# Order of the weight halves for the first batch, and q, k requested ahead of V, in a fused attention and maxout kernel

## Chip, cores and metric

The kernel runs on one core of a Trainium2 chip. The metric is the device time of one execution in microseconds (us), less is better. Profiles are of single executions; their span (first to last instruction) is some 1.8 us shorter than the device time of the same execution.

## The reference, cut to what matters

```python
# q, k, v: [8, 8, 576, 64]
mask = block_i >= block_j                    # blocks of 64 positions
attn = softmax(where(mask, q @ k.T / 8, -1e9))
x = (attn @ v).transpose(0, 2, 1, 3).reshape(4608, 512)
g = maximum(x @ w1, x @ w2)                  # w1, w2: [512, 1024]
out = g @ w_out                              # w_out: [1024, 512]
```

## The kernel before

Attention is worked pair of heads by pair (a "group" g is two pairs; a batch has two groups), in bf16. The second stage (maxout and output projection) has no phase of its own: it is cut into units, and `fill(n)` puts steps of the next unit between the pieces of attention, so that TensorE (PE) has work while DVE, ACT and POOL prepare the next piece. The units form one fixed list. A unit may start when the tokens of its span have been transposed; when the unit at the head of the list may not start, `fill` does nothing. The text calls unit f of span i h(i,f). In the profile's names, ps_o is an attention output before its division, rec and xp the reciprocal and the result of the division, ps_xe and ps_xo the transposes of xp, xT their copy, ps_h a product with w1 or w2, ps_y a row block of the output.

```python
spans = [(0, 256), (256, 320)]               # the two spans of batch 0
spans += [(t0, ...512...) for t0 in range(576, NTOK, 512)]

def h_unit(i, f):                            # 128 of 1024 columns f, span i
    for w_sb in (w1_sb, w2_sb):
        pt = ps_m.tile(...)                  # one of four PSUM banks
        for c in range(4):
            nc.tensor.matmul(pt[:, :w], w_sb[:, c, f*128:(f+1)*128], xT[:, c, t0:t0+w], ...)
        ...                                  # w1: DVE copies to h1;  w2: DVE max(h1, pt) -> g

for i in range(NSPAN):                       # the list
    for f in range(8):
        h(i, f)
        ...
    if i == 1:                               # then ps_y of both spans
        ...

def fill(n):
    while n > 0 and at[0] < len(steps) and steps[at[0]][1] <= done_tokens[0]:
        u, _, cost = steps[at[0]]            # cost 0.5 for 256 columns, 0.625 for 320
        next(u); n -= cost; at[0] += 1
```

The prologue, cut. Every `load_w`, `load_wo`, `load_v` is a transfer issued by POOL that casts to bf16; `load_qk` is issued by SP, released by a small POOL memset ("gated"):

```python
    load_w(256, 256)                         # columns 256..511 of w1 and w2
    ...
    load_w(512, 512)                         # second half of w1 and w2
    ...
    masks_q(1)
    for c in range(3): load_v(1, c)          # V of batch 1
    fill(2)
    load_qk(3, (SP, SP), gated=True)         # q, k of group 3
    burst_q1(2); transposes("q", 2, ...)(); fill(3)
    burst_q2(2); av(0, [2, 3, 4]); fill(1)   # av: attention output, ps_o
    ...
    fill(2); x_out(0, 2, NCH)                # transposes x of group 0 into xT
    ...
    cast("q", 3, pool); cast("k", 3, pool)
    load_qk(4, ...); load_wo(0, 4); load_wo(4, 4)
    fill(3)
    # first turn of the main loop, g == 2
    region(tile_0(a), tile_1(a))
    av(3, [2, 3, 4])                         # last attention output of batch 0
    fill(5)
    x_out(1, 2, NCH)                         # only now span 1 (tokens to 576) may start
    fill(...)
```

The softmax here doesn't subtract the row's maximum and nothing guards it: scores larger than these inputs give would overflow.

## Time and profile before

| | before |
|---|---|
| device time, median of 3 | 282.14 us (282.08 to 282.30) |
| span of the profile | 280.4 us |
| busy: PE, DVE, ACT, POOL | 269.3, 185.7, 139.6, 107.7 us |
| granted PE clock | full |

PE is the engine to watch, and from 18 to 48 us it is fed almost without a break (29.77 of 30.00 us, in the prediction). One more line is needed later, the first matmul of the output projection; columns are start, us from first start to last end, engine, line, operation, operands:

```profile
47.92 0.38 PE L215 MATMUL ps_y<-wo_sb,g 128*128 128x512 bf16 x1
```

I call the time from the first matmul behind the last attention output of batch 0 (28.35 us, the row with x10 in the prediction) to this one **the stretch**: 47.92 - 28.35 = 19.57 us. It is the only part of PE's program that the change permutes.

### The profile page before, as it was taken

The page shows a single profiled execution, that of the slowest core. Times are in us where ns is not written, and L with a number is a line of the kernel's source. Part 1 is how long each engine was busy: PE and PEld are TensorE (multiplying, and loading weights), DVE is VectorE, ACT ScalarE, POOL GpSimd, SP SyncE. Part 2 cuts the span into 40 slices and gives each one's busy share as a digit, 9 for nine tenths or more (in the row PEclk, how much of TensorE's full clock was granted, in tenths as well). Part 3 has the DMA queues.
Part 4 walks back from the last instruction along what each step waited for, and adds up shares of the span by engine and source line. Part 5 has one row for each costly group of instructions (what it writes and reads, how often), then busy time and mean ns, then how long its engine had stood idle before and what let it go on. Part 6 is the DMA issues. An engine that isn't in the chain of part 4 may idle for free.

```text
span 280.4 us, 7767 instructions
## 1 busy us (share of the span) xinstructions
PE 269.3 (96%) x3208; PEld 151.5 (54%) x3253; DVE 185.7 (66%) x386; ACT 139.6 (50%) x194; POOL 107.7 (38%) x271
## 2 busy tenths in 40 slices
PE   7699999999999999999999999999999999999995
PEld 2356766655556455555555554646455644444543
DVE  5967879668887676767667576757655766365430
ACT  3786577667664664655647374664653000100112
POOL 2996446764654625164344625371120000000000
PEclk9999999999999999999999999999999999999999
DMA  7999999979934994479266866175301111111114
GB/s 261 263 219 220 187 244 273 250 148 189 210 42 153 154 156 78 178 82 239 49 208 77 219 75 196 52 81 50 67 5 49 49 54 40 39 75 40 73 41 150
DMA packets 55940, 36.68 MB, mean 131 GB/s; under 512 B 38752, under 2 KB 43232, under 8 KB 55904
## 3 DMA queue, kind: packets, MB, share of 16 engines
q0 software_dynamic: 41728, 7.87, 35.0%
q1 hardware_dynamic: 13760, 27.66, 28.8%
q10 hardware_dynamic: 416, 0.66, 0.7%
q8 instruction: 25, 0.41, 0.6%
q14 instruction: 11, 0.09, 0.1%
HBM read 34.60 MB, written 9.44 MB: 157 GB/s over the span
## 4 chain that ended last, share of the span: by engine, by line
PE 91%; DMA 4%; issue 2%; ACT 1%; DVE 1%; POOL 0%; ACTq 0%
PE ps_h L197 43%; PE ps_y L215 22%; PE ps_o L429 11%; PE ps_s L321 8%; DMA vv<-in_v_dram 2%; PE ps_xe L451 2%; PE ps_qT L303 2%; DMA qraw<-in_q_dram 2%; PE ps_kT L303 2%; ACT aT L345 1%; PE ps_s L339 1%; PE ps_y L231 1%; PE ps_w L292 1%; DVE g L206 0%; POOL vv L133 0%
## 5 line engine op out<-in xcount | busy, mean ns | idle before, releaser
L197 PE MATMUL ps_h<-xT,w_sb 128*128 128x512 bf16 (+3 forms) x605 | 136.2, 357 | 1.7 <-issue 0.3
L345 ACT ACTIVATE aT<-ps_s 128x1024 bf16<-128x1024 f32 (+2 forms) x100 | 96.2, 996 | 17.2 <-PE ps_s L321 16.2
L197 PEld LDWEIGHTS <-w_sb 128*128 128x128 bf16 x640 | 57.8, 98 | 57.4 <-issue 8.1
L204 DVE CAST h<-ps_h 128x512 bf16<-128x512 f32 (+3 forms) x80 | 50.9, 637 | 28.9 <-PE ps_h L197 26.7
L215 PE MATMUL ps_y<-wo_sb,g 128*128 128x512 bf16 x273 | 65.5, 379 | 2.1 <-PE ps_s L321 1.3
L206 DVE TENSOR_TENSOR g<-h,ps_h 128x512 bf16<-128x512 bf16 (+3 forms) x80 | 50.6, 632 | 12.0 <-PE ps_h L197 10.5
L350 POOL MEMSET aT<- 64x128 bf16 x124 | 22.3, 199 | 92.7 <-ACT aT L345 91.3
L221 ACT COPY y<-ps_y 128x512 f32<-128x512 f32 x31 | 18.1, 584 | 70.3 <-PE ps_y L215 56.5
L429 PEld LDWEIGHTS <-aT 128*128 128x128 bf16 x960 | 37.3, 98 | 14.1 <-issue 1.3
L215 PEld LDWEIGHTS <-g 128*128 128x128 bf16 x280 | 26.8, 98 | 30.4 <-issue 1.1
L429 PE MATMUL ps_o<-vv,aT 128*128 128x65 bf16 x960 | 39.9, 194 | 0.3 <-DMA vv<-in_v_dram 0.3
L133 POOL DMA_DIRECT2D vv<-in_v_dram x40 | 33.7, 847 | 0.5
L436 DVE TENSOR_TENSOR xp<-ps_o,rec 128x256 bf16<-128x256 f32 (+1 forms) x64 | 31.4, 491 | 2.2
L321 PE MATMUL ps_s<-qT,kT 64*128 64x64 bf16 (+6 forms) x344 | 31.6, 279 | 1.1 <-ACT kT L310 0.7
L435 DVE RECIPROCAL rec<-ps_o 128x4 f32<-128x4 f32 (+1 forms) x64 | 12.0, 188 | 20.6 <-PE ps_o L429 18.9
L310 ACT COPY qT<-ps_qT 128x576 bf16<-128x576 bf16 x15 | 9.6, 638 | 29.4 <-PE ps_qT L303 29.4
L187 POOL COPY g<-g 128x512 bf16<-128x512 bf16 x8 | 4.9, 611 | 38.3 <-DVE g L206 38.2
L129 POOL CAST kn<-kraw 128x1152 bf16<-128x1152 f32 x15 | 17.3, 1151 | 5.2 <-DMA kraw<-in_k_dram 5.1
L129 POOL CAST qn<-qraw 128x1152 bf16<-128x1152 f32 (+1 forms) x15 | 16.5, 1099 | 7.0 <-DMA qraw<-in_q_dram 6.9
L456 DVE COPY xT<-ps_xe 128x640 bf16<-128x640 bf16 (+2 forms) x18 | 8.2, 453 | 15.7 <-PE ps_xe L451 14.9
L310 ACT COPY kT<-ps_kT 128x576 bf16<-128x576 bf16 x15 | 9.6, 638 | 15.0 <-PE ps_kT L303 15.0
L321 PEld LDWEIGHTS <-kT 64*128 64x128 bf16 x344 | 13.2, 95 | 6.6 <-issue 2.8
(44 smaller groups left out, 144.5 us busy)
## 6 DMA issues: line engine op xcount, KB each, us to landing
qraw<-in_q_dram SPq DMA_DIRECT2D x16, 576.0 KB, 4.1
out_dram<-y SPq DMA_DIRECT2D x35, 256.0 KB, 2.1
kraw<-in_k_dram SPq DMA_DIRECT2D x15, 576.0 KB, 5.4
vv<-in_v_dram POOLq DMA_DIRECT2D x32, 128.0 KB, 5.3
w_sb<-in_moe_w_dram POOLq DMA_DIRECT2D x4, 256.0 KB, 6.6
w_sb<-in_moe_w_dram POOLq DMA_DIRECT2D x2, 512.0 KB, 10.7
wo_sb<-in_moe_w_out_dram POOLq DMA_DIRECT2D x2, 512.0 KB, 11.8
kraw<-in_k_dram ACTq DMA_DIRECT2D x1, 576.0 KB, 5.4
```

The source lines that it names most:

```text
L129: copy(out=n[:, j0:j1], in_=t[:, j0:j1])
L133: nc.gpsimd.dma_start(out=vv_r[b % NV][P - rows:, c, :, :D], in_=v[b, :, c * P:c * P + rows, :].rearrange("h p d -> p h d"),)
L197: nc.tensor.matmul(pt[:, :w], w_sb[:, c, f * P:(f + 1) * P], xT[:, c, t0:t0 + w], start=(c == 0), stop=(c == NDM - 1),)
L204: nc.vector.tensor_copy(out=h1[:, :w], in_=pt[:, :w])
L206: nc.vector.tensor_max(g[:, f, m:m + w], h1[:, :w], pt[:, :w])
L215: nc.tensor.matmul(py[:], g[:, f, s * P:(s + 1) * P], wo_sb[:, f, :], start=(f == 0), stop=(f == NFF - 1),)
L310: copies[i](out=t[:, :S].rearrange("q (p j) -> q p j", j=RPP), in_=pts[i].rearrange("q j p -> q p j"),)
L321: nc.tensor.matmul(ps[:, hh, col:col + w], kT[r, k0:k0 + P], qT[r, q0:q0 + w], start=True, stop=True,)
L345: nc.scalar.activation(out=aT_r[p % NA][:, :, a0:a0 + w], in_=ps[:, :, :w], func=AF.Exp, scale=scale,)
L350: (eng or nc.gpsimd).memset(aT_r[p % NA][BLK:, :, a0:a0 + BLK], 0.0)
L429: nc.tensor.matmul(po[:, gi, hh, :], a[:, hh, a0:a0 + P], vv[:, c, h0 + 2 * hh, :], start=(mm == 0), stop=(mm == n_mm - 1),)
L436: nc.vector.tensor_mul(xp[:, ts[0]:ts[0] + n, :, p % 2], po[:, :, :, :D], rec[:, :n].to_broadcast([P, n, 2, D]),)
```

## The change

Intent: for batch 0, use the first half of the columns of w1 and w2 for both spans before the second half of either, so the second half of the weights may land later; and use that freedom to ask for q and k of group 3 earlier, ahead of V of batch 1.

```diff
-        for i in range(NSPAN):
-            for f in range(NFF):
+        for f0 in (0, NFF // 2):
+            for i in range(2):
+                for f in range(f0, f0 + NFF // 2):
+                    h(i, f)
+        for i in range(1, NSPAN):
+            for f in range(NFF if i > 1 else 0):
                 h(i, f)
...
     masks_q(1)
+    load_qk(3, (SP, SP), gated=True)
     for c in range(3):
         load_v(1, c)
     fill(2)
-    load_qk(3, (SP, SP), gated=True)
```

Below, "part 1" is the order of halves, "part 2" the place of the request. After the change all lines behind 253 are numbered five higher.

## The prediction

> **What bounds the kernel now.** I began with the page of the profile. TensorE (PE) is busy 269.3 of 280.4 us and the granted clock is full in every slice, so it is the suspect, but busy is not the same as fed. The table by stage says where it has room (columns: length, then busy us and instruction count of PE, weight loads, DVE, ACT, POOL, then clock, DMA share, GB/s):
>
> ```profile
> 0.00:18.00 18.00, 13.91 (x178) 6.62 (x181) 13.24 (x41) 10.46 (x14) 12.43 (x25) 1.00 1.26 259
> 18.00:48.00 30.00, 29.77 (x495) 21.28 (x493) 23.66 (x57) 21.45 (x29) 18.46 (x47) 1.00 1.35 228
> 48.00:260.00 212.00, 208.32 (x2441) 114.47 (x2480) 142.41 (x278) 104.01 (x146) 76.81 (x200) 1.00 0.54 110
> ```
>
> The change sits in 18 to 48 us, where PE is busy 29.77 of 30.00. DVE has 6.3 us to spare, ACT 8.5, POOL 11.5. The waits of PE from 18 to 275 us, all of them:
>
> ```profile
> PE ps_y L215 <- PE ps_s L321: 1.3, 8, 0.2
> PE ps_y L215 <- issue: 0.6, 4, 0.2
> PE ps_h L197 <- issue: 0.3, 2, 0.2
> PE ps_xo L453 <- DVE kT L310: 0.2, 1, 0.2
> ```
>
> None is for a weight, for q, k or for V. The first three rows repeat in steps of 0.16 to 0.2 us in places where I count a matmul record missing, so even they are mostly not waits. The change, however, is about when w1, w2, q and k are needed and arrive. Is there a wait hidden inside a matmul? I took the spacing of matmuls instead of their busy time:
>
> ```profile
> 28.35 1.25 PE L197 MATMUL ps_h<-xT,w_sb 128*128 128x256 bf16 x10
> 29.54 0.20 PE L451 MATMUL ps_xe<-ident,xp 64*128 64x64 bf16 x1
> ...
> 35.81 2.35 PE L197 MATMUL ps_h<-xT,w_sb 128*128 128x320 bf16 x16
> ```
>
> Ten of 256 columns: (1.25 - 0.27 of the last) / 9 = 0.109 us apart. Sixteen of 320: (2.35 - 0.30) / 15 = 0.137 us. That is the streaming rate of these shapes; nothing hides in them. I shall use 0.109 and 0.137 below. The first row is also where the second half of w1 and w2 is first used (two matmuls finish f=3, eight are f=4), and it streams.
>
> **What the Trainium skill says.** "Perfetto Trace Analysis", section "Identifying the Most-Contended Engine", warns that busy time of matmuls is no measure of how full PE is; hence the spacing. "TensorE: Matmul & The Clock Gate", section "Back-to-back issue gap", gives an isolated gap of N/2.4 + 2.5 ns: 109 ns at 256 and 136 ns at 320, which this trace meets (109, 137). It also gives about 131 ns for a sustained stream at N=512; this trace does not show that (eleven of them in 2.54 us, (2.54 - 0.38)/10 = 216 ns), and the measurement decides. "DMA: Bandwidth & Descriptors", section "Queues, rings and completion order": each DMA engine serves its queues in turn, a packet at a time. So q, k on SP's queue, requested earlier, take their share from the weights waiting on POOL's queue. In the trace before, the second half of w2 took 11.9 us from issue to landing, the first half 6.1 us; that fits sharing but does not prove it.
>
> **The change, part by part.** No instruction is added or removed: PE has 6508 rows in both programs, DVE 386, POOL 184. I compared the PE order. It is the same up to the last attention output (ps_o) of batch 0, which ends near 28.52 us in the trace before, and the same again from the first output-projection matmul (ps_y) at 47.92 us. Only what lies between is permuted, so the change can only win or lose waits in some 20 us, and shift all that follows by that amount.
>
> *Part 1, order of halves.* Work on batch 0's second span needs the transposed x of its tokens, which the transposes x_out(1) make. Before these, the filler may use the first span only. Formerly that was 64 matmuls; now only the 32 of the first half of w come ahead of the second span. The prologue's fills take 30. The fill of 5 behind the last attention output (5 units at cost 0.5: ten matmuls) now finds two. What happens behind that output on DVE, before:
>
> ```profile
> 28.55 0.20 DVE L435 RECIPROCAL rec<-ps_o 128x6 f32<-128x6 f32 x1 [1.18 <-PE ps_o L429]
> 28.79 0.56 DVE L436 TENSOR_TENSOR xp<-ps_o,rec 128x384 bf16<-128x384 f32 x1
> 29.26 0.41 DVE L206 TENSOR_TENSOR g<-h,ps_h 128x256 bf16<-128x256 bf16 x1
> ...
> 30.45 0.35 DVE L456 COPY xT<-ps_xe 128x384 bf16<-128x384 bf16 x1
> 30.71 0.28 DVE L457 COPY xT<-ps_xo 128x256 bf16<-128x256 bf16 x1
> ```
>
> The ten matmuls covered exactly the reciprocal and multiply (xp done at 28.79 + 0.56 = 29.35). Their removal makes two new waits:
> - PE is done with two matmuls at 28.52 + 0.22 = 28.74 and then needs xp. From DVE's end to a PE start I allow 0.06 us (the copy of kT that PE waited for ended at 24.27, PE began at 24.33). x_out starts at 29.41: about 0.67 us empty.
> - x_out is ten short transposes, issued in about 0.2 us, results by 29.8. DVE then copies at 29.85: 0.35, and the second copy, overlapping by 0.08, ends at about 30.40. The next PE work is now h(1,0), which reads those copies: its first two matmuls (the head pairs of x_out(0)) may go at 29.85, the third waits until 30.45. They occupy 2 x 0.137 = 0.27, so about 0.35 us is empty. Before, h(0,5) stood here and needed nothing new; the copies even queued behind other DVE work till 30.45.
>
> Against this: the kernel before loses a little here too. Around x_out its trace has an xo that starts 0.18 us after the first xe, and about 0.2 us between the last transpose and the next h (0.1 of which is the usual changeover). So follow both to the scores of pair 5 behind the k transposes, which begin at 35.45 in the trace before:
> - Before, from 28.52 to 35.45 PE did 34 matmuls of 256 and 7 of 320: 34 x 0.109 + 7 x 0.137 = 4.67 us of filler.
> - After, third matmul of h(1,0) at 30.45; 13 left before the q transposes: 1.78 + 0.1 changeover, so q at 32.33. Then, as before, 0.84 us of transposes and scores, 15 matmuls of 320 (2.06 us), 0.1, and 0.5 us to the same scores: 35.8. Filler done: 2 x 0.109 + 30 x 0.137 = 4.33 us.
> - Net: 35.8 - 35.45 = 0.35 later, and 0.34 us of filler still owed: +0.7 us. This contains a gain of 0.2 us: before, those scores waited on an ACT exponential ending at 34.37 + 1.02 = 35.39, and by 35.8 ACT is done.
>
> From there to 48 us PE has the same work as before, less the debt, and the buffers turn over at DVE's pace: a unit of eight matmuls of 256 is 0.87 us of PE against two DVE passes of about 0.41, of 320 columns 1.10 against two of 0.49. DVE keeps up, so the 0.7 us stays to the end.
>
> *Part 2, q and k of group 3 ahead of V.* POOL issued three V transfers at 20.30 to 22.94 and SP's requests followed at 23.12 and 23.53. They landed 6.3 and 9.2 us later, at 29.4 and 32.7. Now SP can go at about 20.5; by the same times they would land near 27 and 30. POOL waited 2.44 and 2.07 us for them:
>
> ```profile
> 29.60 1.15 POOL L129 CAST qn<-qraw 128x1152 bf16<-128x1152 f32 x1 [2.44 <-DMA qraw<-in_q_dram]
> 32.82 1.15 POOL L129 CAST kn<-kraw 128x1152 bf16<-128x1152 f32 x1 [2.07 <-DMA kraw<-in_k_dram]
> 33.91 0.10 POOL L118 MEMSET qraw<- 128x1 f32 x1
> 33.94 0.11 POOL L118 MEMSET kraw<- 128x1 f32 x1
> 33.98 1.51 POOL L148 DMA_DIRECT2D wo_sb<-in_moe_w_out_dram  x2
> ```
>
> But PE took the cast q at 31.98 (ready 30.75) and k at 34.75 (ready 33.97): 1.2 and 0.8 us of slack. Part 2 shortens a wait of POOL that PE never felt. Its cost: V is issued about 0.2 us later (landed 31.7 to 36.8, first needed at 39.7), and the second half of w2 (28.3) may land near 29.5. Part 1 is what makes that harmless: that half is now first used at about 36.3. Request wo would go out about 2.5 us earlier. Its second half landed at 34.74 + 14.3 = 49.0, needed near 49.7, so this buys margin, no time. Part 2: 0.
>
> Sum: +0.7 us on 282.14, so 282.85 us.
>
> **Rivals.**
> - *A gain*: the second half of w, or q and k, is really a wait that the records hide, or moves in some executions. For: w2's second half lands at 28.3 and is read from about 29.0; k has 0.8 us. Against: the matmuls stream at 0.109. If true: 281.5 to 282.1.
> - *Waits fully recovered*: DVE and ACT, ahead at 30 us because PE paused, remove later small waits. From 28.5 to 48 us I find about 0.3 us besides the changeovers that could go, and 0.2 of it is in my sum. It would give 282.4 to 282.6.
> - *A chain of further waits*: the pause lets DVE run dry, then the copies of q and k queue with the h passes and hold accumulators (four banks). DVE was busy 16.92 of 19.50 us from 28.5 to 48, so a stretch may turn DVE-bound. This would give 283.3 to 284.
> - *Transfers collide*: earlier q, k push w or V beyond use. The slack of at least 3 us speaks against; 283 to 285 if so.
>
> **Range and chances.** The middle is 282.85. The first two rivals set the low end, the third the high end: 282.3 to 283.6. Two per cent is 5.6 us, eight times my effect, and nothing in a 20 us stretch that is 99% busy can give or cost that. So within 2%: 0.98.
>
> **What would show it.** Right: span near 281.1; PE or its weight load waiting about 0.7 us on the xp multiply behind the last batch-0 output, then h about 0.35 us on the xT copy; first ps_y about 0.7 us later than 47.92; q, k issued near 20.5 with POOL's casts no longer waiting so long; no wait on w in PE. Wrong: first ps_y at or before 47.92, PE waits on a w, V or q/k transfer, or a difference that grows after 48 us.

## The result, and the profile after

Before 282.15 us (282.08 to 282.30, four runs), after 283.12 us (282.92 to 283.20, four runs). The ratio is 1.0033, 95% interval 1.0015 to 1.0050: the mean time of one kernel's fast runs over that of the other's of the same rounds, so not quite the ratio of the medians. Within 2%, a little slower. The span went from 280.4 to 281.3 us.

The table by stage of the kernel after, to be held against the middle row in the prediction (PE 29.77 there):

```profile
18.00:48.00 30.00, 28.83 (x487) 20.73 (x487) 22.92 (x55) 20.27 (x28) 18.50 (x46) 1.00 1.41 229
```

PE is idle 0.94 us more in the same 30 us. Where is told by the waits of PE from 18 to 275 us, all of them (columns: who waited for whom, us in total, times, longest):

```profile
PE ps_xe L456 <- DVE xp L441: 0.7, 1, 0.7
PE ps_h L197 <- DVE xT L462: 0.3, 1, 0.3
PE ps_xo L458 <- DVE kT L315: 0.2, 1, 0.2
```

The third was there before. The first two are new, and the timeline of PE puts them at the last attention output of batch 0:

```profile
28.54 0.38 PE L197 MATMUL ps_h<-xT,w_sb 128*128 128x256 bf16 x2
29.59 0.20 PE L456 MATMUL ps_xe<-ident,xp 64*128 64x64 bf16 x1 [0.67 <-DVE xp L441]
...
29.86 0.45 PE L197 MATMUL ps_h<-xT,w_sb 128*128 128x320 bf16 x2
30.58 1.11 PE L197 MATMUL ps_h<-xT,w_sb 128*128 128x320 bf16 x7 [0.27 <-DVE xT L462]
...
48.74 0.38 PE L215 MATMUL ps_y<-wo_sb,g 128*128 128x512 bf16 x1
```

Ten matmuls have become two; the third of h(1,0) starts 0.57 us behind the second (30.58 less 30.01, the second's start) where 0.137 is the rate, so 0.43 us is lost there, more than the 0.27 that the bracket counts from the modelled end of the matmul. DVE at the same time, against its rows in the prediction:

```profile
28.74 0.20 DVE L440 RECIPROCAL rec<-ps_o 128x6 f32<-128x6 f32 x1 [1.18 <-PE ps_o L434]
28.97 0.56 DVE L441 TENSOR_TENSOR xp<-ps_o,rec 128x384 bf16<-128x384 f32 x1
29.45 0.41 DVE L206 TENSOR_TENSOR g<-h,ps_h 128x256 bf16<-128x256 bf16 x1
29.97 0.36 DVE L461 COPY xT<-ps_xe 128x384 bf16<-128x384 bf16 x1
30.24 0.28 DVE L462 COPY xT<-ps_xo 128x256 bf16<-128x256 bf16 x1
```

The multiply ends at 29.53 and x_out starts at 29.59; the second copy ends at 30.52 and h(1,0) goes on at 30.58. PE now waits for DVE where DVE's work used to lie under matmuls. The stretch is 48.74 - 28.54 = 20.20 us, 0.63 us more than before. The sum closes when start-to-start times are taken instead of brackets: PE loses 0.73 us more ahead of x_out and 0.43 us at the third matmul of h(1,0), but no longer the 0.15 and 0.17 us within and behind the transposes and the 0.21 us at the scores of pair 5 that it lost before; 1.16 - 0.53 = 0.63.

The stretch also begins 0.19 us later than in the profile before. That comes from 20 us, the first long attention output of batch 0; first the kernel before, then the kernel after:

```profile
20.31 0.90 PE L429 MATMUL ps_o<-vv,aT 128*128 128x65 bf16 x24
```

```profile
20.11 1.28 PE L434 MATMUL ps_o<-vv,aT 128*128 128x65 bf16 x24
```

It began 0.20 us earlier and took 0.38 us longer: inside it PE paused at 20.37 and 20.86 us. Chunks 3 and 4 of V of batch 0 landed at 20.5 and 21.0 us, where before they had landed at 20.3 and 20.6. Behind the stretch nothing differs: 232.5 us from the first ps_y to the end in both. So 0.87 us of span = 0.63 (stretch) + 0.19 (before it) + 0.05 (behind it).

Part 2 did what it was to do for POOL. Its casts, against 29.60 and 32.82 us in the prediction:

```profile
28.00 1.15 POOL L129 CAST qn<-qraw 128x1152 bf16<-128x1152 f32 x1 [0.66 <-PE ps_s L326]
31.45 1.15 POOL L129 CAST kn<-kraw 128x1152 bf16<-128x1152 f32 x1 [2.30 <-DMA kraw<-in_k_dram]
```

q was requested at 20.6 and landed at 27.9, k at 21.0 and 31.3. The price is seen in the weights: the second half of w2, issued at 16.4 us as before, took 15.0 us to land instead of 11.9, so it came at 31.4 us instead of 28.3. The two lines are of the second halves of w1 and w2, first in the kernel before, then in the kernel after; the longest is w2's:

```profile
DMA to landing us min/median/max: 9.5/10.7/11.9
```

```profile
DMA to landing us min/median/max: 10.9/12.9/15.0
```

Not all of these 3.1 us are the price of part 2; the runs below sort it out.

### The profile page after: what moved, and what is told of

Same layout as the page of the kernel before. It is cut to its first block, busy times and chain, and to the rows that moved or that the text cites. A ratio compares the mean times of both kernels' runs of the same rounds, so it can differ in the third digit from the quotient of the medians.

```text
span 281.3 us, 7812 instructions
## 1 busy us (share of the span) xinstructions
PE 274.1 (97%) x3253; PEld 151.7 (54%) x3253; DVE 185.7 (66%) x386; ACT 139.7 (50%) x194; POOL 108.0 (38%) x271
## 4 chain that ended last, share of the span: by engine, by line
PE 94%; DVE 3%; POOL 2%; issue 1%; ACT 0%; POOLq 0%
PE ps_h L197 45%; PE ps_y L215 22%; PE ps_o L434 10%; PE ps_s L326 7%; PE ps_w L297 3%; PE ps_qT L308 2%; PE ps_xe L456 2%; PE ps_kT L308 2%; PE ps_y L231 1%; POOL w_sb L145 1%; PE ps_s L344 1%; DVE qT L315 1%; DVE kT L315 0%; DVE qn L129 0%; POOL kn L129 0%
## 5 line engine op out<-in xcount | busy, mean ns | idle before, releaser
L197 PE MATMUL ps_h<-xT,w_sb 128*128 128x512 bf16 (+3 forms) x640 | 141.5, 358 | 0.4 <-DVE xT L462 0.3
L204 DVE CAST h<-ps_h 128x512 bf16<-128x512 f32 (+3 forms) x80 | 50.9, 637 | 29.8 <-PE ps_h L197 27.9
L215 PE MATMUL ps_y<-wo_sb,g 128*128 128x512 bf16 x280 | 66.5, 379 | 0.0
L434 PEld LDWEIGHTS <-aT 128*128 128x128 bf16 x960 | 37.4, 98 | 13.9 <-issue 1.0
L441 DVE TENSOR_TENSOR xp<-ps_o,rec 128x256 bf16<-128x256 f32 (+1 forms) x64 | 31.4, 491 | 2.2
L326 PEld LDWEIGHTS <-kT 64*128 64x128 bf16 x344 | 13.2, 95 | 6.5 <-issue 2.7
```

The source lines that it names most:

```text
L197: nc.tensor.matmul(pt[:, :w], w_sb[:, c, f * P:(f + 1) * P], xT[:, c, t0:t0 + w], start=(c == 0), stop=(c == NDM - 1),)
L204: nc.vector.tensor_copy(out=h1[:, :w], in_=pt[:, :w])
L215: nc.tensor.matmul(py[:], g[:, f, s * P:(s + 1) * P], wo_sb[:, f, :], start=(f == 0), stop=(f == NFF - 1),)
L326: nc.tensor.matmul(ps[:, hh, col:col + w], kT[r, k0:k0 + P], qT[r, q0:q0 + w], start=True, stop=True,)
L434: nc.tensor.matmul(po[:, gi, hh, :], a[:, hh, a0:a0 + P], vv[:, c, h0 + 2 * hh, :], start=(mm == 0), stop=(mm == n_mm - 1),)
L441: nc.vector.tensor_mul(xp[:, ts[0]:ts[0] + n, :, p % 2], po[:, :, :, :D], rec[:, :n].to_broadcast([P, n, 2, D]),)
```

## The experiments

All twelve runs gave the reference's result. On the later chips times scattered more: the kernel before took 282.05 to 285.32 us in its fast rounds (one round of 287.17 counts as slow and is left out). So I lean on the stretch of each profile and give the ratio of times beside it. "Starts" is the start of the stretch.

| run | halves | request of q, k | starts | first ps_y | stretch | ratio to before (95%) |
|---|---|---|---|---|---|---|
| before | old | after V | 28.35 | 47.92 | 19.57 | |
| after | new | ahead of V | 28.54 | 48.74 | 20.20 | 1.0033 (1.0015 to 1.0050) |
| e0_again | new | ahead of V | 28.20 | 48.40 | 20.20 | 1.0003 (0.9981 to 1.0025) |
| e1_part1 | new | after V | 29.45 | 49.65 | 20.20 | 1.0016 (0.9995 to 1.0037) |
| e2_part2 | old | ahead of V | 28.37 | 49.70 | 21.33 | 1.0088 (1.0059 to 1.0117) |
| e3_cover1 | new, f=4 kept first | after V | 28.51 | 48.77 | 20.26 | 1.0023 (0.9996 to 1.0050) |
| e4_cover2 | new, f=4, 5 kept first | after V | 28.45 | 48.07 | 19.62 | 0.9998 (0.9971 to 1.0026) |
| b_again | old | after V | 28.55 | 48.27 | 19.72 | 1.0024 (0.9989 to 1.0059) |
| e8_split | old, weights cut at 640 | after V | 28.63 | 48.20 | 19.57 | 1.0007 (0.9981 to 1.0033) |
| e9_split_gap | as e8, a filler moved | after V | 28.50 | 48.07 | 19.57 | 0.9995 (0.9976 to 1.0013) |
| e5_early_qk | new | 3 us earlier still | 30.17 | 50.37 | 20.20 | 1.0040 (1.0014 to 1.0065) |
| e10_late_w_old | old, weights late | after V | 28.18 | 55.78 | 27.60 | 1.0284 (1.0247 to 1.0321) |
| e11_late_w_new | new, weights late | after V | 28.88 | 53.10 | 24.22 | 1.0115 (1.0075 to 1.0156) |
| e12_late_w_both | new, weights late | ahead of V | 29.40 | 49.59 | 20.19 | 1.0003 (0.9954 to 1.0053) |

From the first ps_y to the end it is 232.5 to 232.6 us in every row (b_again 232.7). So all that these kernels differ by lies in "starts" and "stretch".

### Theory and rival

Theory after the result: part 1 loses 0.63 us by two uncovered waits on DVE; part 2 itself costs or gains nothing *once part 1 is there*; the 0.19 us at 20 us is scatter of transfers. Rival: the early q, k disturb V and the weights, and part 2 is the loss.

### The change once more, and its parts alone

e0_again is the changed kernel.

> The changed kernel once more, on the chip of the next three runs. Theory: 0.7 to 1.0 us slower than before (283.1 us), with the two waits behind the last batch-0 output as in its first trace: about 0.67 us for the multiply, 0.27 to 0.43 for the xT copy. Open: the 0.2 us that the first trace lost before 22 us, where PE waited on chunks 3 and 4 of batch 0's V (landed 20.5 and 21.0 us, before 20.3 and 20.6). If that is scatter of the transfers from run to run, it may be missing here; if it belongs to the early q, k, it is here again.

Stretch 20.20 us again, with the same two waits (0.7 and 0.3), no pause on V this time: the 0.19 us does not always come with the change. The expected time was missed: on this chip before was no faster (median 282.88 against 282.86), its rounds running from 282.39 to 284.43. The interval, -0.5 to +0.7 us, just holds the 0.63 us, so these times neither show nor refute it.

e1_part1 is the first hunk of the diff above without the second.

> Part 1 alone (order of the halves), q, k after V as before. Theory 'part 1 costs, by two uncovered waits': both waits as in the changed kernel, 0.6 to 0.8 us slower than before, so 282.75 to 282.95. If the V wait at 20 to 21 us comes from the early q, k, it is absent here and the difference to the changed kernel is 0.2 us. Rival 'part 2 makes the loss': equal to before, 282.15.

Stretch 20.20 us, the same two waits: part 1 has the whole 0.63. The V question is answered too, against part 2: here, with q, k requested late, PE paused 0.70 us on V (21.0 to 21.7 us). Such pauses, 0 to 0.9 us in all at 20 to 22 us, came in kernels with and without part 2; e11 below, which had asked for neither q, k nor the second half of the weights by then, has one of 0.70 us too. The median, 283.43 us, was 0.5 above the expected range; the excess is in "starts" (29.45), ahead of the part that was edited.

e2_part2 is the second hunk without the first.

> Part 2 alone (q, k of group 3 ahead of V), halves in the old order. My prediction gave part 2 zero, with w2's second half near 29.5 us; the trace of the changed kernel shows it landing at 31.4. In the old order that half is first read near 29.0, so the revised theory is a wait of PE on w2 of 1.5 to 2.4 us and 283.7 to 284.5 us. Rival 'part 2 is free' (as the prediction's sum has it): 282.1 to 282.3.

The rival "part 2 is free" falls. PE's timeline of this kernel, at the second half of f=4:

```profile
31.09 0.61 PE L197 MATMUL ps_h<-xT,w_sb 128*128 128x256 bf16 x4 [1.90 <-DMA w_sb<-in_moe_w_dram]
```

w2's second half was issued at 16.3 and landed 14.7 us later, at 31.0; the old order wanted it at 29.0. The stretch is 21.33, 1.76 us longer than before. So the parts do not add: part 1 alone +0.63, part 2 alone +1.76, both +0.63. The median of the six runs, 285.63 us, is 1.1 us above the expected range; the profile is of the fastest of them (283.95), so the others may have waited longer, which no trace shows.

How much of the later landing is part 2's? With q, k ahead of V and the weights asked for as before, w2's second half took 14.5 to 15.0 us (after, e0, e2). With q, k behind V it took 11.9 to 13.2 us (before, e3, e4, b_again), but 14.3 in e1, where the pieces ahead of it were late too. Counted from the landing of w2's second quarter, the piece before it, which takes out most of that, it came 8.3 to 8.6 us later in the first three and 5.8 to 6.9 us in the other five. So I estimate some 2 us for part 2; the rest is scatter. In the profile before there was 0.7 us between the landing of that half and its first use. Part 1 makes room by moving the use of that half of w2 from about 29 to 37 us.

### Is it the missing cover?

e3 and e4 keep one or two more units of span 0 ahead of span 1, with q, k after V:

```diff
-        for f0 in (0, NFF // 2):
-            for i in range(2):
-                for f in range(f0, f0 + NFF // 2):
-                    h(i, f)
+        FIRST = NFF // 2 + 1        # e3;  + 2 in e4
+        for i, f0, f1 in ((0, 0, FIRST), (1, 0, NFF // 2),
+                          (0, FIRST, NFF), (1, NFF // 2, NFF)):
+            for f in range(f0, f1):
+                h(i, f)
```

> Part 1 with two more first-span units (f=4 and f=5) left ahead of the second span, q, k after V as before. Theory: eight matmuls cover the multiply and eight cover the xT copies, so both waits vanish: within 0.15 us of before (282.0 to 282.3). Rival 'switching between spans or the changed order on DVE costs by itself': still 0.4 us or more slower, with waits elsewhere between 30 and 48 us.

PE's rows at the place of the two waits, the transposes left out:

```profile
28.45 1.25 PE L197 MATMUL ps_h<-xT,w_sb 128*128 128x256 bf16 x10
...
30.15 1.53 PE L197 MATMUL ps_h<-xT,w_sb 128*128 128x256 bf16 x11
```

Stretch 19.62 us, no wait on xp or xT: with sixteen matmuls back in place both waits are gone, and the cost with them, although span 1 still goes ahead of f=6 and 7 of span 0. The order in itself costs no more than the 0.05 us that are left.

> Part 1 with one more first-span unit (f=4) ahead of the second span, q, k after V as before: covers the multiply, leaves the xT copy. Theory: no wait on xp, but PE's third matmul of h(1,0) waits on the xT copy, 0.4 to 0.75 us, as the copies now queue behind two passes of f=4 on DVE; 0.3 to 0.6 us slower than before. Rival 'the first wait is the whole loss': within 0.1 us of before.

As expected the wait on xp is gone and that on the copies has grown, because they now queue behind f=4's passes on DVE (the copies began at 30.61 us in this profile). Two rows of PE:

```profile
30.28 0.45 PE L197 MATMUL ps_h<-xT,w_sb 128*128 128x320 bf16 x2
31.21 0.43 PE L197 MATMUL ps_h<-xT,w_sb 128*128 128x320 bf16 x2 [0.48 <-DVE xT L463]
```

The stretch of 20.26, 0.69 over before, is 0.1 above the range expected, since PE also paused 0.3 us at 29.1 to 29.5 us: w2's second half landed at 29.4 us here, on its own, and f=4 was needed at 29.1. The profile names no wait there; by its time, this is the natural form of the wait that e2 makes.

### How close is the kernel before to that wait?

b_again is the kernel before, unedited.

> The kernel before, to see its trace on a chip of a later day: on the chip of the last four runs it took 282.4 to 284.4 us (median 282.88), not 282.14, and the changed kernel took the same. Theory 'cover against tolerance': transfers land later there, so the old order waits on the second half of w2 at f=4 (about 28.5 to 29.5 us), which the changed order reads 7 us later; expect one such wait of 0.3 to 2 us in executions slower than 282.7 us, none in those near 282.2. Rival: the slower executions lose it before 22 us, on V of batch 0 or the first q, k, which hits both kernels alike.

A miss for the theory in this execution: the profiled run took 282.78 us, slower than 282.7, and shows no wait on w. Its w2 landed at 29.0 us and was read at about 29.2. The loss was elsewhere: 0.20 us in "starts" (the pause on V at 12.5 us was 0.64, 0.51 in the first profile), 0.15 in the stretch, 0.2 behind it. What makes the slower executions of before slow is therefore not settled; the w wait was seen in e3, not in before. One more trace bears on it: up to the stretch, e1 has the program of before, and its w2 landed at 30.7 us. The old order would have read it at 29.45 + 6 x 0.109 = 30.1, so I estimate a wait of 0.6 us for before in such an execution; none was caught.

e8_split changes two calls of the kernel before:

```diff
-    load_w(256, 256)
+    load_w(256, 384)
...
-    load_w(512, 512)
+    load_w(640, 384)
```

> The kernel before with its weights cut at column 640 instead of 512 (256+384+384 instead of 256+256+512), nothing else. f=4 then comes with the second piece; the last piece is first read at f=5, near 30.1 (w1) and 30.5 us (w2) instead of 28.5 and 29.0. Theory 'tolerance without losing cover': no wait on w and no new wait where transfers are fast (equal to before there), and 0.3 to 1 us faster than before where before waits on w2. The second piece of w1 would land about 1 us later, near 22, needed near 22.8. Rival: that piece comes late and PE waits at 23 us instead, 0.3 to 1 us slower.

Stretch 19.57, no wait on w although the last piece of w2 landed at 29.5 us, as late as in e3, where it cost 0.3. The second piece of w1 landed at 22.1 and made PE wait nowhere. So it has margin without losing cover, but the times do not tell it from before.

e9_split_gap is e8 with the filler ahead of `x_out(0, 2, NCH)` raised by one and the last one of the prologue lowered:

```diff
-    fill(2)
+    fill(3)
     x_out(0, 2, NCH)
...
     load_wo(4, 4)
-    fill(3)
+    fill(2)
```

> e8_split, and one unit of filler (two matmuls of 256) moved from the last fill of the prologue to ahead of x_out(0), where every trace so far has PE wait 0.34 us on a DVE copy that frees an accumulator. Theory: that gap shrinks by 0.2 us, so 0.2 us (under 0.1%) faster than e8_split, hardly to be told by time alone; rival: the gap only moves.

The gap did not shrink: 0.21 us inside the filler (at 23.9 us) and 0.43 at the transposes, now on an ACT copy, where e8 lost 0.34 in one place. Stretch unchanged. Its runs were the steadiest (282.32 to 282.85), but with 282.57 for before in the same rounds no gain is shown. No version of mine beats before measurably.

### What is the change good for?

The two halves of the intent can be tested by making the weights late on purpose. In e10 and e11 (and e12) the second half is requested behind the first three V:

```diff
-    load_w(512, 512)
...
     for c in range(3):
         load_v(1, c)
+    load_w(512, 512)
     fill(2)
```

> The kernel before with the request of the second half of w1 and w2 moved behind the first three V transfers of batch 1, some 6 us later; halves in the old order. Theory: PE waits on w1 and w2 at f=4 from about 28.5 us until they land, I estimate 31 to 34 us: stretch from the last batch-0 output to the first output projection 22.5 to 25 us instead of 19.6, 3 to 5 us slower than before. Rival (V, now ahead of w, frees the queue, so w lands as early as before): under 1 us.

Worse than expected, for two reasons: w2 landed later than my estimate of 31 to 34 us, and something came that I had not thought of. PE's timeline:

```profile
34.94 1.04 PE L197 MATMUL ps_h<-xT,w_sb 128*128 128x256 bf16 x4 [4.78 <-DMA w_sb<-in_moe_w_dram]
...
36.34 3.58 PE L197 MATMUL ps_h<-xT,w_sb 128*128 128x256 bf16 x16
```

w2 landed at 34.9 us, after waits of 1.1 and 4.95 us beyond the rate. And then the matmuls are slow: (3.58 - 0.40) / 15 = 0.212 us apart, where before's ten are 0.109. The granted clock shows why, in 40 slices of 7.2 us:

```profile
PEclk9999779999999999999999999999999999999999
```

The clock went down to half during the pause, at 33.0 us, and stayed there for 6.8 us. The stretch is 27.60, 8.0 us over before: the two waits are 6.1 of it, and the half clock is most of the rest (16 x (0.212 - 0.109) = 1.6 us on this row alone).

> The same late request with the new order of halves (q, k after V). Theory: the new order first reads that half near 36 us, so there is no wait on w; the stretch is 20.2 us as in the other kernels of the new order, 0.6 to 0.7 us over before, and 2 to 4 us faster than the same request in the old order. Rival: w or the later q, k of group 3 still come too late and PE waits 0.5 us or more on them between 32 and 37 us.

Half right. No wait on w: the new order rides over it. But the second rival is there too, PE's waits in the stretch:

```profile
PE ps_qT L308 <- POOL qn L129: 2.4, 1, 2.4
PE ps_xe L456 <- DVE xp L441: 0.7, 1, 0.7
PE ps_h L197 <- DVE xT L462: 0.3, 1, 0.3
```

and behind it, on POOL, q that waited for its transfer behind those weights:

```profile
34.04 1.15 POOL L129 CAST qn<-qraw 128x1152 bf16<-128x1152 f32 x1 [6.36 <-DMA qraw<-in_q_dram]
```

q was requested at 24.5 and landed at 33.9. Again the clock was halved, from 35.2 us, at the end of that pause, for 3.4 us. No other trace shows half clock before PE's last matmul. Stretch 24.22.

> Both parts of the change with the second half of the weights requested late, behind q, k and three V transfers. With part 1 alone (e11) PE still lost 2.4 us on the cast q of group 3, which landed at 33.9 us behind those weights. Theory 'the parts belong together': q goes first, so no wait on q; the weights are not read before 36 us and land near 34: stretch 20.2 to 20.4 us, 0.6 to 1.2 us slower than before, against 5.3 (new order alone, span) and 7.9 (old order) for the same late request. Rival: the weights now land after 36.3 us and PE waits there, 1 us or more.

With both parts the stretch is 20.19: q landed 3.9 us after its request at 21.4, the weights at 32.7 (w1) and 35.9 us (w2), read near 37.4. PE's waits in the stretch are the two of the changed kernel and no others:

```profile
PE ps_xe L456 <- DVE xp L441: 0.7, 1, 0.7
PE ps_h L197 <- DVE xT L462: 0.3, 1, 0.3
```

The two parts belong together, then: with the weights requested 5.8 us later the stretch of the old order grows by 8.0 us; with 8.5 us later the changed kernel's grows by nothing beyond its 0.63. (Part 2 alone with late weights was not run. PE also paused 0.9 us on V at 20 to 21 us here, ahead of the stretch and before these weights were requested.)

e5_early_qk moves the request of the changed kernel up to just behind the weights:

```diff
     load_w(512, 512)
+    load_qk(3, (SP, SP), gated=True)
...
     masks_q(1)
-    load_qk(3, (SP, SP), gated=True)
```

> The changed kernel with the request of q, k of group 3 about 3 us earlier still, right behind the second half of the weights (near 17 us). Theory 'transfers share': chunks 3 and 4 of batch 0's V, in flight then, land 0.5 to 2 us later than 20.3 and 20.6, and PE waits on them at 20 to 22 us; the stretch behind stays 20.2 us; 1.2 to 2.5 us slower than before. Rival (V is ahead in its queue and is not held up): as the changed kernel.

q, k were requested at 17.4 and 17.8 us. Chunks 2 to 4 of V took 8.5 to 9.2 us to land, against 7.1 to 7.7 in the profile before; PE paused 0.12 and 0.71 us on them at 20.9 and 21.1 us (the profile puts 0.55 of that down to a mask of POOL's, but PE went on at 21.86, right behind chunk 3 at 21.82, and the mask is of the next pair), and 0.54 beyond the rate on w, at 26.8. The stretch stayed at 20.20, all the loss is in "starts" (30.17); 0.4 us of it, on V at 12.5 us, lies ahead of the moved request. As e1 shows a pause of 0.70 on V and chunks at 8.3 to 8.9 us without any early q, k, this run alone does not prove that the request delayed V; it fits. The wait on w is the clearer sign: the second quarter of w2 took 12.4 us to land here and 7.6 to 8.9 in every other run with that piece.

## Why the prediction was right, point by point

- **Total.** Forecast 282.85 us (282.3 to 283.6), measured 283.12. The sign and the place were right; the size was right for the stretch, and the rest of the measured 0.97 us is scatter (below).
- **Stretch.** Forecast +0.7 us, measured +0.63, and the same 20.20 in e0, e1 and e5.
- **First wait**, on the multiply: forecast 0.67 us, the profile says 0.67 (0.73 start to start). The ten matmuls had covered the reciprocal and the multiply, as said. e3 and e4, which put the cover back, remove it: shown.
- **Second wait**, on the copies: forecast about 0.35, measured 0.43 beyond the rate. e4 removes it: shown.
- **The 0.2 us of recovered ACT wait**: the pause of 0.21 us at the scores of pair 5 (35.45 us before) is gone after. Right.
- **DVE keeps up** from there: no other wait in the stretch. The rival of a chain of further waits did not come.
- **Part 2 = 0**: right for the kernel as changed, but the term under it was mis-sized. I put w2's second half at 29.5 us; it landed at 31.4. I said that part 1 makes this harmless, and e2 confirms it with a number: without part 1 it is 1.76 us. A comparison under it was not like for like: the 6.1 us given for the first half of w2 is its first quarter (the second took 7.6), half the bytes of the piece that took 11.9, so it says nothing on sharing.
- **Counts of rows**: 6508 for PE and 184 for POOL stand in no kept profile. The profiles agree that nothing was added or removed: 3253 weight loads, 386 DVE, 194 ACT and 271 POOL rows in both.
- **Not foreseen**: 0.19 us of the measured 0.97 came from V at 20 us. Pauses of that kind appeared in runs with and without part 2, so it is scatter of transfers, and the forecast was nearer to the mechanism than the first pair of times was. Why transfers scatter between executions stays open.
- **"A gain, if the records hide a wait on w"**: no such wait in the two profiles of before, but the margin is 0.2 to 0.7 us, and e3 fell into it by 0.3. On a chip where the times of before ran to 284.4 us, the two kernels tied. That the change's tolerance made the tie is argued, not shown: the one slow profile of before lost its time elsewhere, and e1's late w2 only makes it likely.

## What to carry to other kernels

A filler's place is worth as much as its amount: before reordering independent work for the sake of a late transfer, count which waits the work covers where it stands, and leave enough at each dependent step (here sixteen matmuls) to cover the chain behind it. Two edits to one transfer schedule can be harmful alone and cheaper together, so test them as a two by two, not one by one. When whole times scatter by more than the effect, find the stretch between two fixed instructions that the edit alone can alter; here, for the changed order, it repeated to 0.01 us where the times spread by 1 us and more.

## What the Trainium skill lacked or had wrong

- "TensorE: Matmul & The Clock Gate", section "What's actually happening", has the clock drop after at least one idle window of about 3.4 us. In e11 a pause of 2.57 us beyond the rate was followed by 3.4 us at half clock; in e2 a pause of 2.07 us was not followed by any. In the 3.4 us ahead of e11's drop, at 35.2 us, PE had worked until 32.8, so the pause that suffices can be shorter than the page's window. The page's binary states agree with these runs (1.0 and 0.5 were the only ones recorded).
- The same page, section "Back-to-back issue gap": about 131 ns per matmul for a sustained stream at N=512. This case shows 216 ns at N=512, 109 at 256, 136 to 137 at 320, the "isolated" formula, in long streams.
- "DMA: Bandwidth & Descriptors", section "Queues, rings and completion order", tells that queues are served in turn, but gives no figure for what a transfer on one queue does to those waiting on another. Here, with 1.15 MB of q and k requested 2.5 us earlier on SP's queue, the second half of w2 on POOL's queue landed 8.3 to 8.6 us behind w2's second quarter (three runs) instead of 5.8 to 6.9 (five runs).
- No page gives the spread of one transfer between executions. Chunks 2 to 4 of V of batch 0, at most 128 KB each, took 7.1 to 7.7 us from issue to landing in the profile before and 8.3 to 8.9 in e1, whose program is the same up to 28 us; PE paused 0 and 0.70 us on them at 20 to 22 us.
